# Block sums of values from half blocks on VectorE, put beside the values by ScalarE; one mask built and copied; weight and query loads two deep

## The chip, the cores and the metric

One core of a Trainium2 chip runs the whole program. TensorE (PE) multiplies, VectorE (DVE) and ScalarE (ACT) work on tiles, GpSimd (POOL) does some elementwise work and SyncE (SP) issues every transfer from memory, one after the other. The metric is the device time of one execution in microseconds (us); lower is better.

## What is computed

An attention with two kinds of keys, followed by two feed-forward layers. For 2 batches, 8 heads, 768 positions and head size 64:

```
k_sum = k.reshape(B, H, nb, 32, D).max(axis=3)
v_sum = v.reshape(B, H, nb, 32, D).mean(axis=3)
scores_l = scale * q @ k.T            # only where |i - j| < 16
scores_s = scale * q @ k_sum.T + log(32)
a = softmax(concat([scores_l, scores_s]))
attn = a @ concat([v, v_sum])
x = attn as (1536, 512)
x = ((x @ w_a) * (x @ w_b)) @ w_out          # 512 -> 1536 -> 512
h = x @ w_in                                 # 512 -> 2048
out = maximum(0.01 * h, h) @ w_out2          # 2048 -> 512
```

Each position thus sees its near neighbours and 24 block summaries: the maxima of the keys and the means of the values of blocks of 32.

## The kernel before, in words

Attention works in 24 groups of 256 queries (four windows of 64) for a pair of heads, two groups to a "pair", 12 pairs in all. For a pair, `k_prep` transposes the keys on TensorE, ScalarE copies them into `kts`, VectorE takes the block maxima into `ks`, and the maxima are copied beside the keys of each window. `scores` makes the products; VectorE adds a mask (`negm`, one of three) and takes the row minimum; ScalarE takes the exponential; `normal` (VectorE) divides; `p_transpose` turns the result; `pv` multiplies it with the window's values `vw`, which carry in 24 partitions the block sums of the values. The result becomes `x` (a rounded part and a rest).

The block sums come from `v_sums`: `load_vb` brings half of a batch's heads (96 blocks) as two tiles of 16 positions each, GpSimd adds them in three operations, VectorE reduces the remaining 8 positions in two. `v_place` (TensorE with the identity) brings the 24 sums of each head to the first partitions, and `put_sums` copies them with GpSimd into `vw` for each pair. This happens four times, two for each batch.

Beside attention run the feed-forward layers, whose weights arrive as 68 pieces of 512 KB (`stage`) and are converted by seven small steps each (`convert`: wr, abs, clamp, shift, join, add, high, rest; two on ScalarE, the others on VectorE). A piece is loaded into one of three `wst` tiles. The tokens come in three chunks of 512. Chunk 0's attention runs first with the first weight pieces, chunk 1's is interleaved with chunk 0's products, chunk 2's with chunk 1's, and from then on only products are left. The code gives the order of a list of steps with due numbers (`add(at, ...)`); a scheduler then orders the instructions of each engine, and each engine works its queue strictly in that order.

At the start GpSimd clears the two `vw` tiles, builds the identity and then the three masks, which differ in 16 columns.

Of the kernel before, what the change touches and what calls it, by code (L numbers as in the profile page):

```python
# [21 lines left out]
def kernel(  # L22
# [12 lines left out]
    nc = tc.nc  # L35
# [30 lines left out]
    M1 = 4  # L66
# [5 lines left out]
    wst_p = ctx.enter_context(tc.tile_pool(name="wst", bufs=3))  # L72
# [7 lines left out]
    q_p = att.enter_context(tc.tile_pool(name="q", bufs=3))  # L80
# [38 lines left out]
    HV = H // 2  # L119
    vb_tiles = []  # L120
    for j in range(2):
        t = xp.tile([P, BLK // 2, D], F32, tag="x", name=f"vb{j}")
        vb_tiles.append(t[0 : HV * NB])
# [26 lines left out]
    def load_vb(b, i):  # L150
        while vb_done[0] in bg:
            bg.pop(0)()
        for j, t in enumerate(vb_tiles):
            nc.sync.dma_start(
                out=t,
                in_=v[b, HV * i : HV * (i + 1)].rearrange("h (n j) d -> (h n) j d", j=BLK)[
                    :, j * (BLK // 2) : (j + 1) * (BLK // 2), :
                ],
            )
# [34 lines left out]
    def put_sums(i, p):  # L194
        for j, b, hp, g, n in runs(p):
            nc.gpsimd.tensor_copy(
                out=vw_of[i][W : W + NB, :, j * G : (j + n) * G, :],
                in_=vs_t[b, 2 * hp // HV][:, 2 * hp % HV : 2 * hp % HV + 2, :]
                .unsqueeze(2)
                .to_broadcast([NB, 2, n * G, D]),  # L200
            )
# [5 lines left out]
    def attention_ops():  # L207
# [3 lines left out]
        for i, p in enumerate(sum(pairs, [])):  # L211
# [4 lines left out]
            for m, (b, hp) in enumerate(dict.fromkeys(x[:2] for x in p)):  # L216
                vi, r = divmod(2 * hp, HV)
                if (b, hp) not in seen:
# [4 lines left out]
                    if r == 0:  # L223
                        add(-4, LOAD, load_vb, b, vi)
                        add(-4, SIDE, v_sums, b, vi)
                        add(7, PRODUCT, v_place, b, vi)
# [16 lines left out]
    for t in vw_t:  # L243
        nc.gpsimd.memset(t, 0.0)
# [4 lines left out]
    ident = const.tile([P, P], F32, tag="ident", name="ident")  # L249
    make_identity(nc, ident)  # L250
    negm = []
    for kind in ("first", "mid", "last"):
        t = const.tile([P, P], F32, tag=f"negm_{kind}", name=f"negm_{kind}")
        nc.gpsimd.memset(t, 0.0)
        nc.gpsimd.memset(t[:, W : W + NB], -math.log(BLK))
        nc.gpsimd.memset(t[:, W + NB : SC], BIG)
        for c in range(2):
            for o, c0, c1 in ((0, 0, W), (W, SC, P)):
                loc = t[c * W : (c + 1) * W, c0:c1]

                nc.gpsimd.affine_select(
                    out=loc, in_=loc, compare_op=ALU.is_ge, fill=BIG,
                    base=o - 1, pattern=[[1, c1 - c0]], channel_multiplier=-1,
                )
                nc.gpsimd.affine_select(
                    out=loc, in_=loc, compare_op=ALU.is_ge, fill=BIG,
                    base=2 * WIN - 1 - o, pattern=[[-1, c1 - c0]], channel_multiplier=1,
                )
        if kind == "first":
            nc.gpsimd.memset(t[:, 0:WIN], BIG)  # L270
        if kind == "last":
            nc.gpsimd.memset(t[:, P - WIN :], BIG)
        negm.append(t)
# [4 lines left out]
    units = [(s, c) for s in range(NF1 // M1) for c in range(NC)]  # L278
    slices2 = [(s * M2 + i, c) for s in range(NF2 // M2) for c in range(NC) for i in range(M2)]
    uses = []  # L280
    for s, c in units:
        fs = range(s * M1, (s + 1) * M1)
        uses += [(nm, f) for f in fs for nm in "ab"] + [("o", f) for f in fs]
# [32 lines left out]
    def convert():  # L316
# [13 lines left out]
        def low():  # L330
            t["r"] = wcv_p.tile([P, 512], I32, tag="wr", name="wr")
# [113 lines left out]
    def v_place(b, i):

        v0, done = vb_t.pop((b, i))
# [3 lines left out]
        for h in range(HV):  # L451
            nc.tensor.matmul(
                out=ps[0:NB, h * D : (h + 1) * D],
                lhsT=ident[0 : HV * NB, h * NB : (h + 1) * NB],
                rhs=v0,
                start=True, stop=True,
            )
        vs = sm_p.tile([NB, HV, D], F32, tag="vs", name="vs", bufs=2)
        nc.scalar.activation(
            out=vs, in_=ps[0:NB, : HV * D].rearrange("p (h d) -> p h d", h=HV),  # L460
            func=AF.Copy, scale=1.0 / BLK,
        )
        vs_t[b, i] = vs

    def k_prep(b, hp, j):

# [366 lines left out]
```

## Time and profile before

| | us |
|---|---|
| median of 3 runs (660.76 to 661.89) | 660.8 |
| the profiled execution, whole | 661.53 |
| its span on the core | 659.8 |
| TensorE busy | 636.2 (96%) |
| VectorE busy | 418.1 (63%) |
| ScalarE busy | 270.8 (41%) |
| GpSimd busy | 48.5 (7%) |

The profiled execution is 1.7 us longer than its span (661.53 against 659.8). Busy shares of the whole say little here: the kernel has a first part of some 100 us with attention, and a long rest of products alone, with other limits.

### The profile page before, as it was taken

The numbers are of one execution on the slowest core, as the hardware profiler recorded it, in microseconds if no ns is written. First come the engines' busy times: TensorE is split into PE (matmuls) and PEld (weight loads), VectorE is DVE, ScalarE is ACT, GpSimd is POOL, SyncE is SP. The second block draws the span as 40 slices with busy tenths as digits, with TensorE's granted clock in tenths as the row PEclk, the third lists the DMA queues.
The fourth block names the chain that finished last, engine by engine and source line by source line (L and its number), as shares of the span: only waits on it lengthen the run. The fifth ranks groups of instructions, "written<-read, shape, count | busy, mean of one in ns | idle before, by whom it ended". The sixth has DMA issues, their size and how long they took to land.

```text
span 659.8 us, 9339 instructions
## 1 busy us (share of the span) xinstructions
PE 636.2 (96%) x3440; PEld 519.3 (79%) x3440; DVE 418.1 (63%) x952; ACT 270.8 (41%) x609; POOL 48.5 (7%) x79
## 2 busy tenths in 40 slices
PE   5797989999999999999999999999999999999997
PEld 4576767777888888888888888888888888888886
DVE  3999889955999962699623869732279532422323
ACT  3776787653545421344222535322255322222221
POOL 7254042000000000000000000000000000000000
PEclk9898999999999999999999999999999999999999
DMA  8997744512334430244200232400013000100101
GB/s 196 232 224 194 171 106 108 149 25 65 128 129 138 149 96 1 64 129 127 65 0 1 67 93 73 152 1 0 1 56 105 1 0 1 64 1 1 64 1 64
DMA packets 72622, 53.43 MB, mean 81 GB/s; under 512 B 46208, under 2 KB 66688, under 8 KB 72576
## 3 DMA queue, kind: packets, MB, share of 16 engines
q1 hardware_dynamic: 72576, 52.84, 28.0%
q8 instruction: 27, 0.44, 0.3%
q14 instruction: 19, 0.16, 0.1%
HBM read 49.68 MB, written 3.15 MB: 80 GB/s over the span
## 4 chain that ended last, share of the span: by engine, by line
PE 88%; DVE 6%; POOL 2%; DMA 1%; issue 1%; SPq 1%; ACT 0%; POOLq 0%; DVEq 0%
PE ps_t L583 38%; PE ps_c L583 18%; PE ps_a L583 14%; PE ps_b L583 13%; PE ps_t L518 2%; PE ps_t L565 1%; DVE pm L545 1%; PE ps_t L553 1%; DMA vb<-in_v_dram 1%; DVE pm L531 1%; POOL vb L425 1%; PE ps_t L472 1%; SPq L182 1%; DVE sm L543 0%; DVE acc L688 0%
## 5 line engine op out<-in xcount | busy, mean ns | idle before, releaser
L583 PE MATMUL ps_t<-x,wsp 128*128 128x512 f32 x336 | 78.4, 389 | 0.0
L583 PE MATMUL ps_c<-wsp,gs 128*128 128x512 f32 x288 | 75.9, 389 | 0.0
L583 PE MATMUL ps_t<-wsp,gs 128*128 128x512 f32 x288 | 74.7, 389 | 0.0
L583 PEld LDWEIGHTS ps_t<-x,wsp 128*128 128x128 f32 x336 | 63.1, 188 | 13.1
L583 PE MATMUL ps_t<-ys,wsp 128*128 128x512 f32 x288 | 71.9, 389 | 0.0
L583 PE MATMUL ps_a<-x,wsp 128*128 128x512 f32 x252 | 66.0, 399 | 1.8 <-ACT x L575 1.0
L583 PE MATMUL ps_b<-x,wsp 128*128 128x512 f32 x252 | 65.3, 395 | 0.0
L583 PEld LDWEIGHTS ps_t<-wsp,gs 128*128 128x128 f32 x288 | 54.0, 188 | 11.3
L583 PEld LDWEIGHTS ps_c<-wsp,gs 128*128 128x128 f32 x288 | 54.1, 188 | 11.2
L583 PEld LDWEIGHTS ps_t<-ys,wsp 128*128 128x128 f32 x288 | 54.1, 188 | 11.2
L583 PE MATMUL ps_c<-gs,wsp 128*128 128x512 f32 x240 | 61.0, 394 | 0.0
L336 ACT ACTIVATE wc<-wst 128x512 f32<-128x512 f32 x68 | 45.7, 674 | 28.9 <-DVE wsp L365 28.8
L362 ACT CAST wsp<-wc 128x512 fp32r<-128x512 f32 x68 | 42.1, 622 | 34.4 <-DVE wc L357 27.5
L583 PEld LDWEIGHTS ps_a<-x,wsp 128*128 128x128 f32 x252 | 46.8, 190 | 11.9 <-ACT x L575 1.3
L790 DVE SCALAR_TENSOR_TENSOR h<-h,ps_t 128x512 f32<-128x512 f32 x24 | 16.5, 686 | 60.3 <-ACT h L789 60.3
L583 PEld LDWEIGHTS ps_b<-x,wsp 128*128 128x128 f32 x252 | 46.6, 189 | 9.5 <-issue 0.3
L365 DVE TENSOR_TENSOR wsp<-wc,wsp 128x512 fp32r<-128x512 f32 x68 | 46.9, 693 | 8.5 <-ACT wsp L362 8.5
L583 PEld LDWEIGHTS ps_c<-gs,wsp 128*128 128x128 f32 x240 | 44.4, 188 | 9.6 <-DVE wr L332 0.2
L357 DVE CUSTOM_DVE_ANT_0 wc<-wc,wr 128x1024 uint16<-128x1024 uint16 x68 | 48.8, 718 | 0.5
L604 DVE TENSOR_TENSOR gs<-h,gs 128x512 fp32r<-128x512 f32 x48 | 33.1, 690 | 22.8 <-ACT gs L603 22.7
L583 PE MATMUL ps_t<-gs,wsp 128*128 128x512 f32 x192 | 47.5, 389 | 0.0
L351 DVE SCALAR_TENSOR_TENSOR wc<-wst,wc 128x512 int32<-128x512 int32 x68 | 46.6, 688 | 0.3
(94 smaller groups left out, 863.5 us busy)
## 6 DMA issues: line engine op xcount, KB each, us to landing
wst<-in_moe_w_out_dram SPq DMA_DIRECT2D x28, 512.0 KB, 3.3
wst<-in_moe_w_in_dram SPq DMA_DIRECT2D x16, 512.0 KB, 3.7
wst<-in_moe_w_a_dram SPq DMA_DIRECT2D x12, 512.0 KB, 4.4
wst<-in_moe_w_b_dram SPq DMA_DIRECT2D x12, 512.0 KB, 3.7
k<-in_k_dram SPq DMA_DIRECT2D x16, 192.0 KB, 3.6
vb<-in_v_dram SPq DMA_DIRECT2D x8, 384.0 KB, 5.4
out_dram<-acc SPq DMA_DIRECT2D x12, 256.0 KB, 2.0
q<-in_q_dram SPq DMA_DIRECT2D x16, 128.0 KB, 2.9
```

Of the source, the lines that this page charges most:

```text
L182: nc.sync.dma_start(out=t[p0 : p0 + o1 - o0, c, w0:w1, :], in_=src)
L336: nc.scalar.activation(out=t["c"].bitcast(F32), in_=hi_w.bitcast(F32), func=AF.Abs)
L351: nc.vector.scalar_tensor_tensor(out=t["c"], in0=hi_w, scalar=-0x40000000, in1=t["c"], op0=ALU.bitwise_and, op1=ALU.bitwise_or,)
L357: nc.vector.tensor_tensor(out=t["c"], in0=t["c"], in1=t["r"], op=ALU.add)
L362: nc.scalar.copy(out=t["w"][:, 0], in_=t["c"].bitcast(F32))
L365: nc.vector.tensor_tensor(out=t["w"][:, 1], in0=t["c"].bitcast(F32), in1=t["w"][:, 0].bitcast(F32), op=ALU.subtract,)
L425: nc.gpsimd.tensor_tensor(out=a, in0=a, in1=b, op=ALU.add)
L472: nc.tensor.transpose(ps[:, i * P : (i + 1) * P], k2[:, g * (GT // P) + i].rearrange("p c d -> p (c d)"), ident)
L518: nc.tensor.matmul(out=ps[h, w, :], lhsT=qt[h, w * W : (w + 1) * W], rhs=kts[h, (g * G + w) * SC : (g * G + w) * SC + P], start=True, stop ...
L583: nc.tensor.matmul(out=ps, lhsT=w(a), rhs=x(b), start=first and j == 0, stop=last and j == 2)
L604: nc.vector.tensor_tensor(out=t[:, 1], in0=src, in1=t[:, 0].bitcast(F32), op=ALU.subtract)
L790: nc.vector.scalar_tensor_tensor(out=h, in0=h, scalar=0.01, in1=ps, op0=ALU.mult, op1=ALU.max)
```

## The change

1. Block sums: `load_vb` now brings a whole batch at once as three tiles of 128 half blocks (16 positions each); VectorE reduces each tile alone in two operations; TensorE adds the two halves of a block while it places them, with a constant matrix `place`. There are two such rounds instead of four; GpSimd's adds are gone.
2. `put_sums` moves from GpSimd to ScalarE, the copy of the block maxima into `kts` from GpSimd to VectorE.
3. One mask is built by GpSimd; VectorE copies it for the other two and sets 16 columns. The identity is made first, and `vw` is cleared later.
4. To make room, `wst` has two tiles instead of three, the query tiles two instead of three, and `wr` one instead of two.

The M1 lines of the change keep the same groups of four.

```
-    wst_p = ctx.enter_context(tc.tile_pool(name="wst", bufs=3))
+    wst_p = ctx.enter_context(tc.tile_pool(name="wst", bufs=2))
-    q_p = att.enter_context(tc.tile_pool(name="q", bufs=3))
+    q_p = att.enter_context(tc.tile_pool(name="q", bufs=2))
...
+    NV = 2 * H * NB // P
+    vb_tiles = [xp.tile([P, BLK // 2, D], F32, tag="x", name=f"vb{j}") for j in range(NV)]
...
-    def load_vb(b, i):
+    def load_vb(b):
...
+        src = v[b].rearrange("h (n j) d -> (h n) j d", j=BLK // 2)
+        for i, t in enumerate(vb_tiles):
+            nc.sync.dma_start(out=t, in_=src[i * P : (i + 1) * P])
...
-            nc.gpsimd.tensor_copy(
+            nc.scalar.copy(
                 out=vw_of[i][W : W + NB, :, j * G : (j + n) * G, :],
...
+    for i, c0 in ((0, 0), (2, P - WIN)):
+        nc.vector.tensor_copy(out=negm[i], in_=t)
+        nc.vector.memset(negm[i][:, c0 : c0 + WIN], BIG)
...
-            t["r"] = wcv_p.tile([P, 512], I32, tag="wr", name="wr")
+            t["r"] = wcv_p.tile([P, 512], I32, tag="wr", name="wr", bufs=1)
...
+        v0 = sm_p.tile([P, NV, D], F32, tag="v0", name="v0", bufs=1)
         ops = [
-            lambda: add(t0[:, 0:h], t1[:, 0:h]),
-            lambda: add(t0[:, h:], t1[:, h:]),
-            lambda: add(t0[:, 0:h], t0[:, h:]),
+            lambda i=i, d=d: nc.vector.tensor_reduce(
+                out=v0[:, i, d : d + D // 2],
+                in_=vb_tiles[i][:, :, d : d + D // 2].rearrange("p j d -> p d j"),
+                op=ALU.add, axis=AX.X,
+            )
+            for i in range(NV)
+            for d in (0, D // 2)
         ]
...
+        for h in range(H):
+            r0, r1 = 2 * h * NB, 2 * (h + 1) * NB
+            tiles = range(r0 // P, (r1 - 1) // P + 1)
+            for i in tiles:
+                c0 = V0 + (r0 - i * P) // 2
+                nc.tensor.matmul(
+                    out=ps[0:NB, h * D : (h + 1) * D],
+                    lhsT=place[:, c0 : c0 + NB],
+                    rhs=v0[:, i],
+                    start=i == tiles[0], stop=i == tiles[-1],
+                )
...
-            nc.gpsimd.tensor_copy(
+            nc.vector.tensor_copy(
                 out=kts[:, 0:NW, W : W + NB],
```

VectorE in the first microseconds of the program, before: behind the mask additions of the first pair (L531) the two reduces of the value sums (L435) follow, and key maxima (L482) of a later pair of heads.

```order
L531 ISA nb 128x1
L435 TENSOR_REDUCE v_244<-vb_101 96x32 x2
L482 TENSOR_REDUCE ks_97<-ps_t_326 128x16
L482 TENSOR_REDUCE ks_97<-ps_t_347 128x8
L543 TENSOR_SCALAR sm<-sm 128x4
L544 RECIPROCAL sm<-sm 128x4
L545 TENSOR_TENSOR pm<-pm,sm 128x512
L332 TENSOR_SCALAR wr<-wst 128x512
```

The same engine with the change, from the end of the first group's mask additions: the reduces of the first tile of half blocks stand there already, ahead of the second group.

```order
L528 ISA nb 128x1
L428 TENSOR_REDUCE v_198<-vb_101 128x32 x2
L479 TENSOR_REDUCE ks_96<-ps_t_199 128x16
L540 TENSOR_SCALAR sm<-sm 128x4
L479 TENSOR_REDUCE ks_96<-ps_t_207 128x8
L541 RECIPROCAL sm<-sm 128x4
L486 COPY kts_92<-ks_96 128x12x24
L542 TENSOR_TENSOR pm<-pm,sm 128x512
L528 ISA pm,nb<-ps_t_258,negm_mid 128x128
```

Of six reduces for the batch two stand between the first two groups, and the other four behind the second; the copies into `kts` stand on VectorE right behind the maxima.

SyncE's queue before, from the queries of the fourth pair on: the second half of batch 0's value blocks, then queries ahead, keys, and the fourth weight piece (`wst`); the first three were issued earlier.

```order
L142 DMA q<-in_q_dram 128x4x64 x2
L154 DMA vb_101<-in_v_dram 96x1024
L154 DMA vb_102<-in_v_dram 96x1024
L142 DMA q<-in_q_dram 128x2x64 x8
L133 DMA k<-in_k_dram 128x6x64 x2
L310 DMA wst<-in_moe_w_b_dram 128x4x256
L182 DMA vw_99<-in_v_dram 48x64 x2
```

With the change the same stretch holds all of batch 1's value blocks, and the weight piece there is the third; only two were issued ahead of it.

```order
L141 DMA q<-in_q_dram 128x4x64 x2
L154 DMA vb_101<-in_v_dram 128x1024
L132 DMA k<-in_k_dram 128x6x64 x2
L154 DMA vb_102<-in_v_dram 128x1024
L154 DMA vb_103<-in_v_dram 128x1024
L141 DMA q<-in_q_dram 128x2x64 x4
L177 DMA vw_99<-in_v_dram 48x64 x2
L315 DMA wst<-in_moe_w_a_dram 128x4x256
L177 DMA vw_99<-in_v_dram 64x7x64 x2
```

Batch 1's blocks moved ahead of the third and later weight pieces, and the third piece moved behind the fourth pair's queries.

## Rows read from the trace of the kernel before

**Rows 1.** Busy time of each engine by stretch: us, engines' busy us, PEclk, DMA, GB/s

```profile
0.00:10.00 10.00, 4.18 (x20) 3.44 (x22) 2.73 (x16) 3.85 (x10) 8.52 (x45) 1.00 0.86 207
10.00:62.00 52.00, 40.73 (x409) 31.15 (x406) 47.36 (x156) 34.40 (x120) 23.24 (x19) 0.92 0.86 211
62.00:98.00 36.00, 33.10 (x341) 26.62 (x340) 30.57 (x104) 27.31 (x94) 10.47 (x13) 0.97 0.58 145
300.00:400.00 100.00, 100.00 (x443) 82.81 (x442) 62.66 (x115) 35.29 (x59) 0.00 (x0) 1.00 0.19 58
```

**Rows 2.** The chain that ended last: start us, us, what

```profile
9.22 0.42 POOL kts L489
...
9.71 1.99 PE ps_t L518 x16
...
11.82 0.29 DVE pm L531
...
33.71 3.39 POOL vb L425 x2
...
60.58 0.69 PE ps_t L472 x2
...
97.12 0.73 PE ps_a L583 x2
```

**Rows 3.** VectorE's groups from 0 to 62 us: count, busy us, mean ns, idle before

```profile
L545 DVE TENSOR_TENSOR pm<-pm,sm 128x512 f32<-128x512 f32 x9 | 9.5, 1054 | 0.1
L357 DVE CUSTOM_DVE_ANT_0 wc<-wc,wr 128x1024 uint16<-128x1024 uint16 x6 | 5.4, 893 | 0.0
L332 DVE TENSOR_SCALAR wr<-wst 128x512 int32<-128x512 uint32 x6 | 3.3, 553 | 0.0
L543 DVE TENSOR_SCALAR sm<-sm 128x4 f32<-128x4 f32 x9 | 2.9, 326 | 1.6 <-ACT pm L535 1.6
```

**Rows 4.** The same groups later: L545 and L543 98:160, others 220:400

```profile
L545 DVE TENSOR_TENSOR pm<-pm,sm 128x512 f32<-128x512 f32 x8 | 5.5, 689 | 0.1
L543 DVE TENSOR_SCALAR sm<-sm 128x4 f32<-128x4 f32 x8 | 1.3, 164 | 1.1 <-ACT pm L535 1.1
...
L357 DVE CUSTOM_DVE_ANT_0 wc<-wc,wr 128x1024 uint16<-128x1024 uint16 x23 | 15.8, 688 | 0.3
L332 DVE TENSOR_SCALAR wr<-wst 128x512 int32<-128x512 uint32 x23 | 9.7, 422 | 0.6 <-DMA wst<-in_moe_w_in_dram 0.5
```

**Rows 5.** Two of the groups from 62 to 98 us

```profile
L545 DVE TENSOR_TENSOR pm<-pm,sm 128x512 f32<-128x512 f32 x7 | 5.7, 808 | 0.1
L543 DVE TENSOR_SCALAR sm<-sm 128x4 f32<-128x4 f32 x7 | 2.0, 293 | 0.4 <-ACT pm L535 0.4
```

**Rows 6.** Groups from 0 to 160 us that price what is moved

```profile
L435 DVE TENSOR_REDUCE v<-vb 96x32 f32<-96x256 f32 x8 | 4.5, 589 | 0.3 <-POOL vb L425 0.3
L482 DVE TENSOR_REDUCE ks<-ps_t 128x16 f32<-128x512 f32 x8 | 5.4, 679 | 6.3 <-ACT kts L479 6.3
L482 DVE TENSOR_REDUCE ks<-ps_t 128x8 f32<-128x256 f32 x8 | 3.3, 416 | 0.0
L196 POOL COPY vw<-vs 24x1024 f32<-24x1024 f32 x8 | 12.4, 1563 | 47.4 <-PE ps_t L565 44.3 <-ACT vs L459 3.1
L477 ACT COPY kts<-ps_t 128x384 f32<-128x384 f32 x8 | 3.8, 473 | 6.6 <-PE ps_t L472 6.6
L477 ACT COPY kts<-ps_t 128x192 f32<-128x192 f32 x8 | 2.5, 315 | 0.0
```

**Rows 7.** VectorE in order of time: first key maxima; the fourth x

```profile
6.13 1.02 DVE L482 TENSOR_REDUCE ks<-ps_t 128x16 f32<-128x512 f32 x2 [4.65 <-ACT kts L479]
...
63.95 0.69 DVE L576 TENSOR_TENSOR x<-ps_t,x 128x512 fp32r<-128x512 f32 x1
```

**Rows 8.** SyncE's issue of the fourth weight piece; loads' time to landing, from the page

```profile
33.39 0.48 SPq L310 DMA_DIRECT2D wst<-in_moe_w_b_dram  x1
...
wst<-in_moe_w_a_dram SPq DMA_DIRECT2D x12, 512.0 KB, 4.4
```

More of the change, by code (lines that the diff above doesn't have):

```diff
@@ L222, in attention_ops @@
                         add(2 * m + j - 12, PRODUCT, k_prep, b, hp, j)
[L223 to L226, printed above, removed]
+                    if hp == 0:
+                        add(-5, LOAD, load_vb, b)
+                        add(-4, SIDE, v_sums, b)
+                        add(7, PRODUCT, v_place, b)
             add(-14, LOAD, load_q, i, p)
@@ L240, in by_window @@
         return t[:, at : at + NW * SC].rearrange("p (w o) -> p w o", o=SC)
-    for t in vw_t:
-        nc.gpsimd.memset(t, 0.0)
+    ident = const.tile([P, P], F32, tag="ident", name="ident")
+    make_identity(nc, ident)
     for t in kts_t:
@@ L248 @@
         nc.vector.memset(by_window(t)[:, :, W + NB :], 0.0)
[L249 to L253, printed above, removed]
-        nc.gpsimd.memset(t, 0.0)
[L255 to L273, printed above, removed]
@@ L278 @@
-    units = [(s, c) for s in range(NF1 // M1) for c in range(NC)]
+    negm = [
+        const.tile([P, P], F32, tag=f"negm_{kind}", name=f"negm_{kind}")
+        for kind in ("first", "mid", "last")
+    ]
+    t = negm[1]
+    nc.gpsimd.memset(t, 0.0)
+    nc.gpsimd.memset(t[:, W : W + NB], -math.log(BLK))
+    nc.gpsimd.memset(t[:, W + NB : SC], BIG)
+    for c in range(2):
+        for o, c0, c1 in ((0, 0, W), (W, SC, P)):
+            loc = t[c * W : (c + 1) * W, c0:c1]
+            nc.gpsimd.affine_select(
+                out=loc, in_=loc, compare_op=ALU.is_ge, fill=BIG,
+                base=o - 1, pattern=[[1, c1 - c0]], channel_multiplier=-1,
+            )
+            nc.gpsimd.affine_select(
+                out=loc, in_=loc, compare_op=ALU.is_ge, fill=BIG,
+                base=2 * WIN - 1 - o, pattern=[[-1, c1 - c0]], channel_multiplier=1,
+            )
@@ new lines @@
+    for i, c0 in ((0, 0), (2, P - WIN)):
+        nc.vector.tensor_copy(out=negm[i], in_=t)
+        nc.vector.memset(negm[i][:, c0 : c0 + WIN], BIG)
+    for t in vw_t:
+        nc.gpsimd.memset(t, 0.0)
+    V0 = 32
+    place = const.tile([P, P], F32, tag="place", name="place")
+    nc.gpsimd.memset(place, 1.0 / BLK)
+    for base, pattern, mult in ((2 * V0, [[-2, P]], 1), (1 - 2 * V0, [[2, P]], -1)):
+        nc.gpsimd.affine_select(
+            out=place, in_=place, compare_op=ALU.is_ge, fill=0.0,
+            base=base, pattern=pattern, channel_multiplier=mult,
+        )
@@ L279 @@
+    assert sum(M1) == NF1
+    group1 = [range(sum(M1[:s]), sum(M1[: s + 1])) for s in range(len(M1))]
+    units = [(s, c) for s in range(len(M1)) for c in range(NC)]
     slices2 = [(s * M2 + i, c) for s in range(NF2 // M2) for c in range(NC) for i in range(M2)]
@@ L281 @@
     for s, c in units:
-        fs = range(s * M1, (s + 1) * M1)
-        uses += [(nm, f) for f in fs for nm in "ab"] + [("o", f) for f in fs]
+        uses += [(nm, f) for f in group1[s] for nm in "ab"] + [("o", f) for f in group1[s]]
     behind = []
@@ L450, in v_place @@
         ps = at_bank()
[L451 to L463, printed above, removed]
+        for h in range(H):
[3 more added lines that the diff above has]
+                c0 = V0 + (r0 - i * P) // 2
+                assert 0 <= c0 <= P - NB
+                nc.tensor.matmul(
[3 more added lines that the diff above has]
+                    start=i == tiles[0], stop=i == tiles[-1],
+                )
+        vs = sm_p.tile([NB, H, D], F32, tag="vs", name="vs", bufs=2)
+        nc.scalar.copy(out=vs, in_=ps[0:NB].rearrange("p (h d) -> p h d", h=H))
+        vs_t[b] = vs
     def k_prep(b, hp, j):
@@ L641 @@
             o[2]()
[L642 removed]
+            if o[1] == PRODUCT and (bg or cnt["conv"] < N_FIRST) and o[0] > 0:
                 tick(2)
@@ L701, in y_products @@
     def y_products(s, c, gs):
-        ws = [weights(("o", s * M1 + i)) for i in range(M1)]
+        ws = [weights(("o", f)) for f in group1[s]]
+        n = len(ws)
         def add(ps, e, i):
@@ L732 @@
     for s, c in units:
-        todo = range(len(gs), M1)
+        todo = group1[s][len(gs) :]
         pace["bg"] = {(0, 0): 4, (0, 1): 1, (0, 2): 3}.get((s, c), 1.3)
```

58 lines of the change are left out of this document (16 added, 42 removed).

## The prediction

> **What bounds the kernel now.** I read busy time by stretch first. From 300 to 400 us TensorE is busy 100.00 of 100 us at full clock and VectorE 62.66 [rows 1]; there nothing that VectorE, ScalarE or the loads save can show. Only the front can gain. From 10 to 62 us VectorE is busy 47.36 of 52 us, the transfers 0.86 of their time, TensorE 40.73; from 62 to 98 us TensorE has 33.10 of 36 us, VectorE 30.57 [rows 1]. TensorE's busy time overstates its work in the front, where short products stand apart from each other. So the question is by how much the point from which TensorE never waits again comes earlier; every microsecond there goes through to the end, because the rest is products back to back.
>
> The chain that ended last says what leads to that point. It starts on GpSimd, which works through `vw`, the identity and three masks; the first copy of key maxima is queued behind them and runs at 9.22 us, though VectorE had the maxima by 7.15 us (6.13 plus 1.02) [rows 2, 7]. The first scores follow at 9.71 and the first mask addition at 11.82 us [rows 2]. Later the chain passes through GpSimd's value sums at 33.71 us, then VectorE's queue until TensorE starts again at 60.58 us; a second stretch of VectorE's work ends at 97.12 us, and from there on the chain is TensorE [rows 2]. I therefore cut the front into two stages: up to the fourth `x` of chunk 0 (63.95 us, [rows 7]), and from there to 97 us.
>
> The third thing to see is that VectorE's operations are longer while GpSimd works. GpSimd is busy 23.24 us between 10 and 62 us and not at all from 300 to 400 [rows 1]. The normalising product takes 1054 ns on average up to 62 us and 689 ns from 98 to 160; the small addition before it 326 against 164 ns; `add` of the conversion 893 against 688; `wr` 553 against 422 [rows 3, 4].
>
> **The change part by part, first stage.**
>
> Start: the copy into `kts` moves to VectorE, directly behind the maxima. The keys' arrival sets their transposes and does not change. The copy ends at about 7.15 + 0.42 = 7.57 us (GpSimd's own price) instead of 9.64, so all behind it starts 2.1 us earlier. The one mask is needed by 9.7 us; GpSimd has a third of the mask work left and clears `vw` between, so I cost it at nothing, and VectorE's two mask copies fall into its idle start (2.73 us busy in the first 10 [rows 1]). **−2.1.**
>
> GpSimd gone from VectorE's side: nine products at 1054 − 689 = 0.365 (3.3 us), nine small additions at 0.162 (1.5), six `add` at 0.205 (1.2), six `wr` at 0.131 (0.8) [rows 3, 4]. **−6.8.** It could be nothing only if something other than GpSimd stretched them; the same lines at their short durations, where GpSimd rests, speak against it.
>
> Reduces: four of 256 elements in two rounds go, six of 512 come for the batch. A reduce of 256 in this strided form takes 0.589 us, and two in a row start about 0.5 apart. From 256 to 512 elements the contiguous reduce grows by 679 − 416 = 0.263 us [rows 6]: 0.5 + 0.27 = 0.77 each. If the whole were to double, 1.0 each. I take 0.77, since the growth with length is what the rows show directly: 6 × 0.77 − 4 × 0.5 = **+2.6** (with 1.0: +4.0). The Trainium skill, "VectorE: DVE Perf Modes", says in its tier table that a reduce has only the one-element-per-cycle form, and in the section on the errata that the fixed part is about 150 cycles; an estimate by it for 512 elements is 0.69 us, and the sum over both stages would be about 1 us better. Its formula gives 0.42 us for the reduce of 256, against 589 ns measured, so the measurement decides.
>
> Copies into `kts`: four of 288 elements per batch. VectorE has no such row; the reduce of 256 takes 0.42 and `wr` of 512 also 0.42 undisturbed [rows 4, 6]. Between half and all of that: 0.36 each, **+1.4** (0.8 to 1.7).
>
> Conversions: in the new order two closing steps and one `add` of weight pieces that stood ahead of the fourth `x` now stand behind it, 3 × 0.6: **−1.8** here, +1.8 in the second stage.
>
> `put_sums` on ScalarE: a copy grows by (473 − 315) / 192 = 0.82 ns per element [rows 6], so 1024 elements cost 0.473 + 640 × 0.82 ns = 1.0 us (1.56 on GpSimd). Four pairs and the next two waiting make 6 us in this stage, where ScalarE is idle for 52 − 34.40 = 17.6 us [rows 1]. Each copy stands behind the `x` that frees its tile, so it waits for nothing new; behind it are exponentials and key copies. I cost it at nothing; if its cover were gone, 6 us. The 20 placing products against 16 before, some 0.1 us each, are nothing for the same reason.
>
> Loads: this is the price to set against the gain. Up to the fourth weight piece SyncE had issued 7.45 MB in 33.39 us [rows 8], 223 GB/s, which is near what all stretches up to 62 us show (207 and 211, with 0.86 busy [rows 1]). So transfers pace the queue. With two `wst` tiles the third weight piece is no longer fetched early; 8.27 MB stand ahead of it by the shapes in the queue, 1.57 MB of them batch 1's value blocks. It goes out at 8.27 / 0.223 = 37.1 us and lands 4.4 us later [rows 8], 41.5. VectorE's queue up to that piece's `wr`, summed by kinds from the first mask addition (seven groups of mask additions 5.9, six reduces 4.6, three maxima 2.8, three copies 1.1, six normalisations 5.1, two conversions 5.6, two `x` 1.2), is 26.3 us; from 9.7 it is there at 36.0 if nothing waits, so it waits up to 5.5 us. Behind `wr` stand the next mask additions and normalisations; ScalarE's `abs` of that piece waits likewise with exponentials behind it. VectorE's own old idle time of 52 − 47.4 = 4.6 us in this stretch returns here in part. I take **+3.0** (0 to 5.5).
>
> Sum of the first stage: −2.1 − 6.8 + 2.6 + 1.4 − 1.8 + 3.0 = **−3.7**.
>
> **Second stage.** Relief from GpSimd: seven products at 808 − 689 (0.8) and seven additions at 293 − 164 (0.9) [rows 4, 5], −1.7. Batch 1's reduces +2.6, its copies +1.4, the moved conversions +1.8: +4.1. VectorE is idle 36 − 30.57 = 5.4 us here [rows 1], most of it while TensorE sets the pace, and the new reduces stand in that part; about half of it absorbs 2.8. **+1.3.** ScalarE gets 4 us more at 8.7 us idle. With neither cover it is +4.1.
>
> Sum: −3.7 + 1.3 = **−2.4 us**. Against the profiled execution that is 661.5 − 2.4 = 659.1; it lies 0.7 above the median of the runs, so for a median of runs 660.8 − 2.4 = **658.4**.
>
> **The rivals.**
>
> *The loads decide, slower.* The third, fourth and fifth weight pieces each arrive late on an in-order VectorE. For: transfers are already 0.86 busy, and 1.57 MB not needed before 65 us go first. Against: the fourth piece has less ahead of it than VectorE's queue gains meanwhile. Price: 5.5 us at the third piece, 2.5 again at the fifth, 8.0 instead of 3.0, so +2.6 in the end: 663.4. It decides when the third piece lands more than about 5.5 us after VectorE asks for it.
>
> *VectorE only trades.* Reduces at 1.0 each add 1.4 in each stage, and the idle time of the second absorbs little: −2.4 + 2.8 = +0.4, 661.2. For: the strided reduce is already dearer than its length. Against: the growth per element is known.
>
> *Both covers hold.* No new wait for loads (−3.0) and all of the second stage absorbed (−1.3): −6.7, 654.1. For: VectorE idles in the second stage as long as TensorE leads; against: transfers are near their rate.
>
> **How the numbers follow.** 0.2% is 1.3 us, about what a measurement of this kernel can tell from no change. My forecast (−1.4 to −5) has a chance of 0.45, both covers 0.10, the trade 0.20, the loads 0.25. Faster 0.55, within 0.2% 0.20, slower 0.25. The range goes from a little below the case in which both covers hold, 653.5, to a little above that of the loads, 664.0. The likeliest one's own range is 655.8 to 659.4.
>
> **What would show it.** The first mask addition near 9.7 us; the normalising product near 690 ns in the front; reduces of 0.8 to 0.9 us each, twelve of them; `put_sums` near 1.0 us on ScalarE; a wait of VectorE's `wr` for the third weight piece around 37 to 41 us; the fourth `x` near 60 us; TensorE without gaps from about 94 us. The prediction fails if `wr` or `abs` waits are much longer than 3 us together, if ScalarE becomes full from 20 to 60 us, or if TensorE gets gaps behind 100 us from the two-deep loads.

## The result: slower, 667.39 us against 661.35

| | before | after |
|---|---|---|
| median | 661.35 | 667.39 |
| runs | 660.76 to 662.15 (4) | 667.03 to 667.46 (4) |
| span of the profiled execution | 659.8 | 665.3 |

The ratio is 1.0089 with a 95% interval of 1.0070 to 1.0107. The forecast was 658.4; the time lies above its range (653.5 to 664.0) and on the side of the rival "the loads decide, slower" (663.4), beyond that too.

Busy time by stretch, after, the same stretches as [rows 1] (us, then PE, PEld, DVE, ACT, POOL busy, PEclk, DMA, GB/s):

```profile
0.00:10.00 10.00, 4.61 (x28) 3.93 (x29) 2.77 (x22) 2.87 (x6) 5.23 (x22) 1.00 0.86 227
10.00:62.00 52.00, 42.29 (x417) 32.56 (x416) 44.74 (x164) 42.55 (x138) 0.00 (x0) 0.93 0.77 203
62.00:98.00 36.00, 28.36 (x269) 22.06 (x269) 29.10 (x93) 23.69 (x75) 0.00 (x0) 0.91 0.43 111
...
300.00:400.00 100.00, 100.00 (x443) 82.81 (x442) 62.99 (x115) 33.84 (x56) 0.00 (x0) 1.00 0.20 64
```

Nothing changed from 300 to 400 us. Up to 62 us VectorE is less busy, 44.74 against 47.36, and ScalarE more, 42.55 against 34.40. From 62 to 98 us every engine is *less* busy than before: TensorE 28.36 instead of 33.10. Nobody is full; somebody waits for somebody. That is where the time went.

VectorE after, in order of time: the first mask addition, batch 0's second row of reduces, and the fourth `x`, which closes the first stage ([rows 2, 7] for before):

```profile
9.77 0.29 DVE L528 CUSTOM_DVE_ANT_0 pm<-ps_t,negm_first 128x128 f32<-128x128 f32 x1 [2.15 <-PE ps_t L515]
...
15.29 3.81 DVE L428 TENSOR_REDUCE v<-vb 128x32 f32<-128x512 f32 x4
...
60.63 0.66 DVE L573 TENSOR_TENSOR x<-ps_t,x 128x512 fp32r<-128x512 f32 x1
```

The fourth `x` came at 63.95, now at 60.63: the first stage gained 3.3 us, where −3.7 was forecast. The span grew by 5.5 (665.3 − 659.8), so all behind the fourth `x` lost 8.8, where +1.3 was forecast.

The chain that ended last, after, through that loss (start us, us, what):

```profile
64.69 0.03 SPq L315
64.72 0.03 issue
64.75 5.79 DMA wst<-in_moe_w_b_dram
...
70.63 0.07 ACT wc L341
70.69 0.50 issue
71.19 0.61 ACT gs L600
71.80 0.02 issue
71.83 0.69 DVE gs L601
...
75.21 1.29 DVE v L428 x2
...
77.95 2.82 DVE v L428 x3
80.77 0.08 DVE sm L540
80.85 0.59 DVE wc L356
81.44 0.08 DVE sm L540
81.52 0.60 DVE ks L479
82.12 0.04 issue
82.17 0.69 PE ps_t L469 x2
```

Read it downwards. A weight piece is issued at 64.75 and lands at 70.5. ScalarE's `abs` (L341) of that piece stands at the head of its queue, and behind it the cast of `gs` (L600), whose data are ready; VectorE's `gs` (L601) waits for that cast. Then VectorE works off mask additions and batch 1's six reduces (L428) in one row, and only behind them the key maxima (L479) that free the PSUM bank which TensorE needs next. What TensorE sees of it:

```profile
75.59 0.71 PE L580 MATMUL ps_b<-x,wsp 128*128 128x512 f32 x2
82.17 0.69 PE L469 MATMUL ps_t<-ident,k 128*128 128x128 f32 x2 [5.87 <-DVE ks L479]
82.83 1.97 PE L515 MATMUL ps_t<-kts,qt 64*64 64x128 f32 x16
...
89.26 1.09 PE L515 MATMUL ps_t<-kts,qt 64*64 64x128 f32 x16
```

It stands for 5.87 us, and the sixteen score products right behind the gap take 1.97 us instead of 1.09: the granted clock is 0.81 on average from 80 to 98 us and 0.50, the lower of the two levels, from 82 to 86. From 62 to 98 us TensorE idles 36 − 28.36 = 7.6 us (2.9 before), and the clock, 0.91 against 0.97, takes at most another 36 × 0.06 = 2.2 (an estimate; part of the slow time falls into the gap itself). Together up to 4.7 + 2.2 = 6.9 of the 8.8; the rest this view does not place.

The kernel before has a gap of the same kind, at the end of its first stage, and there too the clock falls behind it (0.50 from 62 to 64 us):

```profile
60.58 0.69 PE L472 MATMUL ps_t<-ident,k 128*128 128x128 f32 x2 [3.91 <-DVE ks L482]
```

The change took that gap away and put a longer one later. TensorE's last wait ends at 91.97 us now and at 97.12 us before, so the point from which it never waits again did come earlier. The kernel is slower all the same, because TensorE had less behind it by then: up to 98 us it was busy 4.61 + 42.29 + 28.36 = 75.3 us, before 78.0, which is half of the 5.5 us.

### The profile page after: what moved, and what is told of

The parts are those of the page before. It is cut to its first block, busy times and chain, and to the rows that moved or that the text cites. A ratio compares the mean times of both kernels' runs of the same rounds, so it can differ in the third digit from the quotient of the medians.

```text
span 665.3 us, 9283 instructions
## 1 busy us (share of the span) xinstructions
PE 638.8 (96%) x3448; PEld 520.3 (78%) x3448; DVE 417.3 (63%) x968; ACT 281.6 (42%) x623; POOL 5.2 (1%) x22
## 4 chain that ended last, share of the span: by engine, by line
PE 89%; DVE 5%; ACT 2%; DMA 2%; issue 1%; POOL 1%; SPq 0%; POOLq 0%; ACTq 0%; DVEq 0%
PE ps_t L580 37%; PE ps_c L580 18%; PE ps_a L580 13%; PE ps_b L580 13%; PE ps_t L515 3%; DMA wst<-in_moe_w_b_dram 2%; DVE v L428 1%; PE ps_t L562 1%; PE ps_t L550 1%; ACT pm L532 1%; DVE pm L528 1%; PE ps_t L497 1%; DVE wc L356 0%; DVE acc L685 0%; DVE pm L542 0%
## 5 line engine op out<-in xcount | busy, mean ns | idle before, releaser
L341 ACT ACTIVATE wc<-wst 128x512 f32<-128x512 f32 x68 | 45.7, 675 | 52.9 <-DMA wst<-in_moe_w_out_dram 12.1
L601 DVE TENSOR_TENSOR gs<-h,gs 128x512 fp32r<-128x512 f32 x48 | 33.1, 691 | 22.8 <-ACT gs L600 22.7
L362 DVE CUSTOM_DVE_ANT_0 wc<-wc,wr 128x1024 uint16<-128x1024 uint16 x68 | 46.6, 685 | 0.6
```

The costliest lines, as they stand in the source:

```text
L341: nc.scalar.activation(out=t["c"].bitcast(F32), in_=hi_w.bitcast(F32), func=AF.Abs)
L362: nc.vector.tensor_tensor(out=t["c"], in0=t["c"], in1=t["r"], op=ALU.add)
L601: nc.vector.tensor_tensor(out=t[:, 1], in0=src, in1=t[:, 0].bitcast(F32), op=ALU.subtract)
```

## The experiments

Three things in the changed kernel can lengthen that stretch: the two `wst` tiles (**late pieces**), batch 1's six reduces (**the row**), and `put_sums` on **ScalarE**. The first theory was the row, its rival the late pieces; ScalarE came third. All ratios are against the kernel before on the same chip. A summary first (the wait is TensorE's longest between 62 and 98 us of the profiled execution, with what ended it; the kernels marked * leave work out). "Cast" is ScalarE's step that writes a converted weight piece to `wsp`, "closing step" VectorE's last step on it.

| run | ratio, 95% interval | longest wait, us | ended by |
|---|---|---|---|
| the changed kernel | 1.0089 (1.0070–1.0107) | 5.87 | key maxima |
| three deep | 0.9980 (0.9968–0.9992) | 2.95 | key maxima |
| batch 1 reuses sums * | 1.0006 (0.9983–1.0028) | 1.62 | cast |
| early reduces | 1.0011 (0.9995–1.0027) | 3.82 | cast |
| before, two deep | 1.0012 (0.9995–1.0028) | 1.2 | `x` |
| three deep + reuse * | 0.9914 (0.9880–0.9947) | under 0.2 | – |
| three deep, row split | 0.9971 (0.9948–0.9993) | 1.23 | key maxima |
| put_sums on GpSimd | 0.9993 (0.9973–1.0013) | 2.72 | closing step |
| before, new start | 0.9993 (0.9973–1.0013) | 1.0 | normalising product |
| no late put_sums * | 1.0031 (1.0015–1.0047) | 6.75 | cast |
| q three deep | 1.0040 (1.0020–1.0059) | 5.82 | cast |
| three deep + put_sums on GpSimd | 0.9985 (0.9973–0.9998) | 3.61 | key maxima |
| the same, row split | 0.9977 (0.9962–0.9992) | 1.23 | key maxima |
| three deep, batch 1 folded on GpSimd | 1.0034 (1.0021–1.0047) | 2.92 | cast |
| two deep, batch 1 folded on GpSimd | 1.0077 (1.0057–1.0096) | 2.69 | cast |
| three deep, folded, put_sums on GpSimd | 0.9893 (0.9869–0.9917) | 0.4 | – |
| three deep, folded, batch 1's put_sums on GpSimd | 0.9919 (0.9894–0.9945) | 0.7 | normalising product |
| two deep, folded, put_sums on GpSimd | 0.9962 (0.9950–0.9974) | 1.30 | normalising product |
| three deep, folded, put_sums on GpSimd, again | 0.9924 (0.9901–0.9947) | 0.4 | – |

**Row or late pieces.** Three deep:

```
-    wst_p = ctx.enter_context(tc.tile_pool(name="wst", bufs=2))
+    wst_p = ctx.enter_context(tc.tile_pool(name="wst", bufs=3))
```

> The changed kernel with three wst tiles again instead of two (q stays at two, wr at one). Block theory (batch 1's six reduces stand in one row on VectorE ahead of the key maxima that free TensorE's banks; TensorE stands for 5.87 us and its clock falls behind that): the row of reduces is still there, so TensorE still waits 4 to 6 us at the key transposes, and the time is 664 to 667. Load theory (the weight pieces that go out late, landing at 57.5 and 70.5 us, leave VectorE and ScalarE idle, and the reduces only fill the hole): no wait of abs for wst over 0.5 us between 50 and 75 us, and the time falls to 657 to 661.

Batch 1 takes batch 0's sums:

```
 def v_sums(b):
+    if b:
+        vb_t[b] = vb_t["first"]
+        return
...
-    vb_t[b] = v0, ops[-1]
+    vb_t[b] = vb_t["first"] = v0, ops[-1]
```

> The changed kernel without the six reduces of batch 1, which takes batch 0's sums again (work left out; the loads of batch 1's value blocks stay). Block theory: TensorE's wait of 5.87 us at 76 us is under 1.5 us, the clock stays at 1.00 from 80 to 100 us, and the time falls by 6 to 9 us, to 658 to 661. Load theory: VectorE waits for the late weight pieces as before and the reduces were filler: 665 to 667.5. Their bare price of 12 halves by twelve, 6 x 0.93 = 5.6 us, would give 661.8 if VectorE alone set the pace.

Batch 1's load and reduces earlier:

```
-    add(-5, LOAD, load_vb, b)
-    add(-4, SIDE, v_sums, b)
+    add(-5 - 12 * b, LOAD, load_vb, b)
+    add(-4 - 12 * b, SIDE, v_sums, b)
```

> The changed kernel with batch 1's load of value blocks and its six reduces due 12 steps earlier, so that the reduces stand between 133 and 157 of VectorE's queue in pieces of one to three instead of in one row at 210. No work is left out. Block theory: TensorE's wait before the key transposes shrinks to under 2 us, part of the 5.6 us of reduces is paid in the first stage instead (fourth x 2 to 5 us later than 60.63), clock stays full from 80 to 100: 660 to 664. Load theory: the late pieces still leave their holes, and the first stage is longer: 667 to 670.

The kernel before with only the tiles cut:

```
-    wst_p = ctx.enter_context(tc.tile_pool(name="wst", bufs=3))
+    wst_p = ctx.enter_context(tc.tile_pool(name="wst", bufs=2))
...
-    q_p = att.enter_context(tc.tile_pool(name="q", bufs=3))
+    q_p = att.enter_context(tc.tile_pool(name="q", bufs=2))
...
-            t["r"] = wcv_p.tile([P, 512], I32, tag="wr", name="wr")
+            t["r"] = wcv_p.tile([P, 512], I32, tag="wr", name="wr", bufs=1)
```

> The kernel before with only the loads two deep: two wst tiles, two q tiles, one wr tile. Block theory: the loads cost little by themselves, 660 to 663. Load theory: abs and wr wait for wst as in the changed kernel, 5 us or more in 50 to 75 us, and the time is 665 to 669. The prediction's own term was +3.0 (0 to 5.5) in the first stage.

Neither theory had it alone. Three deep gave back 0.0109 of the time (7.2 us of 661), though the row is still there; no reduces gave back 0.0083 (5.5, to 662.84 us, between the two theories' ranges), though the pieces are as late as before. TensorE with three deep:

```profile
74.50 1.64 PE L580 MATMUL ps_b<-x,wsp 128*128 128x512 f32 x6
79.08 0.44 PE L469 MATMUL ps_t<-ident,k 128*128 128x128 f32 x2 [2.95 <-DVE ks L479]
```

The same place, half the wait: VectorE comes to the row at 72.02 instead of 75.13. And ScalarE without the reduces:

```profile
66.76 0.67 ACT L341 ACTIVATE wc<-wst 128x512 f32<-128x512 f32 x1 [2.42 <-DMA wst<-in_moe_w_a_dram]
70.76 0.66 ACT L341 ACTIVATE wc<-wst 128x512 f32<-128x512 f32 x1 [2.34 <-DMA wst<-in_moe_w_b_dram]
```

The late piece stops `abs` as in the changed kernel, and yet TensorE waits 1.62 us at most. So the gap of 5.87 is two delays behind each other on VectorE's queue, less TensorE's work in hand, and the clock fell on top: 0.81 from 80 to 98 us in the changed kernel, 1.00 with three deep, 0.91 without the reduces. Early reduces do all the work, and in time (663.31 us, 1.0011) and in the wait for key maxima, which is gone, they do as row theory said. Not as it said are the fourth `x`, no later than before (60.68), and a new wait:

```profile
78.11 1.22 PE L580 MATMUL ps_b<-x,wsp 128*128 128x512 f32 x2 [3.82 <-ACT wsp L367]
```

That is the cast of a weight piece whose `abs` had waited 2.64 us for its load. In the kernel before, two deep is not told from nothing in time, though an `abs` waits for its piece there too (1.38 us at 76.03).

**Do they add up, and is a split row better.** Three deep and reuse joined:

```
-    wst_p = ctx.enter_context(tc.tile_pool(name="wst", bufs=2))
+    wst_p = ctx.enter_context(tc.tile_pool(name="wst", bufs=3))
...
 def v_sums(b):
+    if b:
+        vb_t[b] = vb_t["first"]
+        return
...
-    vb_t[b] = v0, ops[-1]
+    vb_t[b] = vb_t["first"] = v0, ops[-1]
```

> The changed kernel with three wst tiles and without batch 1's six reduces (it takes batch 0's sums again; work left out). Taken alone the two edits gave back 6.6 and 4.6 us. Separate costs: the two add up, 655 to 657. One gap (the late piece and the row of reduces stand in a row ahead of the same key maxima, TensorE has some microseconds of cover, and whatever is taken off first ends the gap): little more than the better of the two, 658 to 660.5, with no wait of TensorE over 1.5 us between 70 and 85 us.

Three deep, and batch 1's load and reduces due 4 steps earlier:

```
-    wst_p = ctx.enter_context(tc.tile_pool(name="wst", bufs=2))
+    wst_p = ctx.enter_context(tc.tile_pool(name="wst", bufs=3))
...
-    add(-5, LOAD, load_vb, b)
-    add(-4, SIDE, v_sums, b)
+    add(-5 - 4 * b, LOAD, load_vb, b)
+    add(-4 - 4 * b, SIDE, v_sums, b)
```

> The changed kernel with three wst tiles and batch 1's reduces due 4 steps earlier; they stand as four and two in VectorE's queue instead of six in a row. No work is left out. Row theory (what is left of TensorE's wait at the key transposes with three tiles, 2.95 us, comes from the six standing in one row): that wait is under 1 us and the time 657 to 660. If only the amount of VectorE's work counts: 660 to 662, as with three tiles alone.

Joined: 656.90 us, ratio 0.9914, against 1.0089 a gain of 0.0175; the single gains sum to 0.0192 (by the ratios; the 6.6 and 4.6 us of the forecast are differences of the bare times). They add up, or nearly, and not in "one gap". With the row split into four and two the wait at the key transposes is 0.70 us, the longest 1.23; 659.77 us, but its interval overlaps that of three deep alone.

**ScalarE, and the start.** `put_sums` back on GpSimd:

```
-            nc.scalar.copy(
+            nc.gpsimd.tensor_copy(
                 out=vw_of[i][W : W + NB, :, j * G : (j + n) * G, :],
```

> The changed kernel with put_sums on GpSimd again, loads still two deep. ScalarE theory (the 12 copies of 0.6 to 1.0 us that went to ScalarE delay the abs and the exponentials, and so the stall): 660 to 664. If ScalarE's added work is off the path, as the prediction has it (costed at nothing): 666 to 670, the copies on GpSimd stretching VectorE's operations in the front by some 2 us in all.

The kernel before with the start of the change alone (identity first, one mask built, `vw` cleared behind it):

```
...
+    for i, c0 in ((0, 0), (2, P - WIN)):
+        nc.vector.tensor_copy(out=negm[i], in_=t)
+        nc.vector.memset(negm[i][:, c0 : c0 + WIN], BIG)
...
-            nc.gpsimd.tensor_copy(
+            nc.vector.tensor_copy(
                 out=kts[:, 0:NW, W : W + NB],
```

> The kernel before with the new start alone: identity first, one mask built and copied, vw cleared behind it, the copy of key maxima into kts on VectorE. The prediction's terms: first mask addition at 9.7 us instead of 11.82, -2.1 and up to +1.4 for the copies; GpSimd's block sums stay. 658.5 to 660.5. If what is won at the start is lost again in the waits of the front: 660.5 to 662.

GpSimd's `put_sums` gave back 0.0096 (6.3 us) with the loads still two deep, as ScalarE theory said. But the edit moved other things too: the six reduces stand as three, two and one on VectorE there, and up to 96 us `abs` waits only once for a piece, 0.81 us. So this run does not separate ScalarE's share from the other two. The new start alone: the first mask addition at 9.54 us as forecast, the fourth `x` at 64.78 (63.95 before), no gain that can be told. VectorE is busy 50.17 of 52 us from 10 to 62 us there (47.36 before); that a head start is used up ahead of such a full engine is the likely reading, which no run tests.

**Controls.** `put_sums` for the first two pairs only; and `q` instead of `wst` three deep:

```
 def put_sums(i, p):
+    if i > 1:
+        return
```

> The changed kernel with put_sums for the first two pairs only; the windows of later pairs keep those sums (work left out). Nothing goes to GpSimd in its place. If ScalarE's copies set the pace of the first stage from 40 to 56 us, as moving them to GpSimd showed (fourth x at 57.61 instead of 60.63), the fourth x is at 57 to 58.5 us here too and the time 659 to 662. If that gain came from another order of the queues or from GpSimd, the fourth x stays at 60 to 61 and the time at 665 to 668.

```
-    q_p = att.enter_context(tc.tile_pool(name="q", bufs=2))
+    q_p = att.enter_context(tc.tile_pool(name="q", bufs=3))
```

> The changed kernel with three q tiles again; wst stays at two, and the six reduces still stand in one row. It separates the depth of the weight tiles from that of the query tiles, and is a control for a mere change of order. If the weight tiles are the cause: abs still waits for wst 2 us or more in 50 to 75 us, and the time is 665 to 668. If query loads at the head of SyncE's queue held the weight pieces back: 659 to 662.

Without late `put_sums` the fourth `x` is at 57.38 as ScalarE theory said, though the time, 664.12 us, is above its range; but with `q` three deep, and ScalarE's copies in place, it is at 58.10: the fourth `x` is not proof against ScalarE. (In the changed kernel the conversion of a late piece stands ahead of it; in these two it fell behind.) Both keep two `wst` tiles and the reduces, five or six in a row, and both keep a gap as long, 6.75 and 5.82 us, but another operation ends it. With `q` three deep:

```profile
78.00 1.22 PE L580 MATMUL ps_b<-x,wsp 128*128 128x512 f32 x2 [5.82 <-ACT wsp L367]
```

Here it is the `add` of a weight piece that stands on VectorE behind the row (71.04 to 76.70), and the cast behind that `add`. The row delays whatever stands behind it; which operation that is depends on the order. The control also bounds what a third query tile and the changed order that comes with it are worth together: some 3 us (665.70, ratio 1.0040 against 1.0089). It does not tell the one from the other.

**Joined with ScalarE.** Three deep and `put_sums` on GpSimd, then the same with the row split:

```
-    wst_p = ctx.enter_context(tc.tile_pool(name="wst", bufs=2))
+    wst_p = ctx.enter_context(tc.tile_pool(name="wst", bufs=3))
...
-            nc.scalar.copy(
+            nc.gpsimd.tensor_copy(
                 out=vw_of[i][W : W + NB, :, j * G : (j + n) * G, :],
```

> The changed kernel with three wst tiles and put_sums on GpSimd; the row of six reduces stays. Alone the two edits gave back 7.2 and 6.3 us. If the late piece and ScalarE's copies are separate costs: 654 to 657. If both cure the same stall: 659 to 661.

```
-    add(-5, LOAD, load_vb, b)
-    add(-4, SIDE, v_sums, b)
+    add(-5 - 4 * b, LOAD, load_vb, b)
+    add(-4 - 4 * b, SIDE, v_sums, b)
```

> As the last one, with batch 1's reduces due 4 steps earlier, so that they stand as four, one and one in VectorE's queue. All work is done. Row theory: 1 to 3 us faster than the last one; if only the amount of VectorE's work counts: the same within 1 us.

Not separate this time: 661.63 and 661.21 us, no better than three deep alone. In the first the row is still there, and TensorE waits 3.61 us for the key maxima behind it; in the second the row is split and the wait is 1.23 us, and the time is the same within 1 us, against row theory. With GpSimd's copies (7.65 us from 10 to 62 us) VectorE is busy 48.08 us in that stretch, against 45.91 with three deep alone.

**All the work done without the row.** Batch 1's sums folded on GpSimd, with three and with two `wst` tiles:

```
 def v_sums(b):
...
+    if b:
+        def fold(i, n):
+            t = vb_tiles[i]
+            nc.gpsimd.tensor_tensor(
+                out=v0[:, i] if n == 1 else t[:, 0:n],
+                in0=t[:, 0] if n == 1 else t[:, 0:n],
+                in1=t[:, 1] if n == 1 else t[:, n : 2 * n], op=ALU.add,
+            )
+        ops = [lambda i=i, n=n: fold(i, n) for i in range(NV) for n in (8, 4, 2, 1)]
     bg[0:0] = ops
```

> The changed kernel with three wst tiles, and batch 1's block sums folded on GpSimd (twelve additions of 512, 256, 128 and 64 elements) instead of VectorE's six reduces; batch 0's stay on VectorE, put_sums on ScalarE. All work is done. If the two causes of the stall (late pieces, row of reduces) are what the changed kernel lost, this comes near the run that had three tiles and no reduces of batch 1 (0.9914): 655 to 658, no wait of TensorE over 1.5 us between 62 and 85 us. If GpSimd stretches VectorE as much as it relieves it, it stays at the 0.998 of three tiles alone, 659.5 to 661.5.

> The same folding on GpSimd with two wst tiles, as in the changed kernel: only the late pieces stay. If each cause makes some 3 us of TensorE's gap of 5.87 us: a wait of TensorE of 1.5 to 3.5 us between 70 and 82 us, and 661 to 664. If the late pieces alone make the whole stall: 665 to 668.

With three tiles this was to come near 0.9914 and came to 1.0034 (665.11 us): the theory of two causes fell. With two tiles it is slower still, 668.79 us, above both forecasts: `abs` waits 1.78 and 2.22 us for pieces there, TensorE 2.12 us at the key transposes (78.92) and 2.69 us for a cast. So the late pieces stop TensorE without the row too, and cost 3.7 us in this pair. With three tiles the gap at the key transposes is gone, and a new one stands at 88.51. ScalarE with three deep and folding:

```profile
83.49 0.62 ACT L191 COPY vw<-vs 24x512 f32<-24x512 f32 x1
...
84.62 0.62 ACT L191 COPY vw<-vs 24x512 f32<-24x512 f32 x1
...
85.78 0.61 ACT L191 COPY vw<-vs 24x512 f32<-24x512 f32 x1
...
87.20 0.62 ACT L191 COPY vw<-vs 24x512 f32<-24x512 f32 x1
87.84 0.62 ACT L367 CAST wsp<-wc 128x512 fp32r<-128x512 f32 x1
```

and TensorE:

```profile
88.51 1.22 PE L589 MATMUL ps_a<-x,wsp 128*128 128x512 f32 x2 [2.92 <-ACT wsp L367]
```

VectorE finished that piece's `add` at 84.07 (83.38 + 0.69); its cast waits behind exponentials and four copies to 87.84. In the run with three deep and reuse, which has the same copies on ScalarE, the cast stood ahead of them:

```profile
77.26 0.62 ACT L367 CAST wsp<-wc 128x512 fp32r<-128x512 f32 x1
...
86.10 2.18 ACT L191 COPY vw<-vs 24x512 f32<-24x512 f32 x4
```

Same operations, same engine, and no wait: what counts is which queued operation stands behind them. The last question was then put to two kernels, with all or only batch 1's `put_sums` on GpSimd:

```
-            nc.scalar.copy(
+            nc.gpsimd.tensor_copy(
                 out=vw_of[i][W : W + NB, :, j * G : (j + n) * G, :],
```

> Three wst tiles, batch 1's block sums folded on GpSimd, and put_sums on GpSimd too; all work is done. The run before it (three tiles, folding, put_sums on ScalarE) had no gap of TensorE at the key transposes any more but a new one of 2.92 us at 88 us, behind four put_sums copies of 0.62 us on ScalarE, and lay at 1.0034. If ScalarE's copies are that next limit: no wait of TensorE over 1.5 us between 80 and 95 us, and 657 to 661. If GpSimd's work brings VectorE's long operations back by as much: 662 to 665.

```
-            nc.scalar.copy(
+            (nc.gpsimd.tensor_copy if b else nc.scalar.copy)(
                 out=vw_of[i][W : W + NB, :, j * G : (j + n) * G, :],
```

> The same, but only batch 1's put_sums on GpSimd; batch 0's stay on ScalarE, so that the first stage is as in the run before it. If ScalarE's copies of batch 1 are the next limit: the gap of 2.92 us at 88 us gone and 660 to 663; if not: 664 to 666.

0.9893 and 0.9919 (656.44 and 657.99 us, both below their forecasts): with these queues ScalarE's copies of batch 1 are a third cost. They are not one in every order: three deep + reuse leaves them on ScalarE and stands at 0.9914. TensorE waits nowhere over 0.8 us between 62 and 98 us, and the clock there is 1.00 in both. Both do all the work and are faster than the kernel before. With the first as a base the loads can be priced once more, two deep beside three deep:

```
-    wst_p = ctx.enter_context(tc.tile_pool(name="wst", bufs=3))
+    wst_p = ctx.enter_context(tc.tile_pool(name="wst", bufs=2))
```

> As the run with batch 1's sums and put_sums on GpSimd, but with two wst tiles as in the changed kernel: only the two-deep loads are left of the three suspects. If late weight pieces are a cost of their own: abs waits for wst 1.5 us or more at least once between 50 and 75 us, and the time lies 3 to 7 us above the three-deep run beside it. If they cost only together with the row of reduces or with ScalarE's copies: within 1.5 us of it.

> Three wst tiles, batch 1's block sums and put_sums on GpSimd, once more, beside the two-deep one on the same chip: 0.987 to 0.992 of before, as measured first (0.9893).

Side by side 659.60 and 656.79 us, with intervals that do not meet: two deep costs 2.8 us here. That late pieces do it, this pair does not show. Its forecast for late pieces as a cost was a wait of `abs` of 1.5 us or more between 50 and 75 us; the only wait of `abs` for a piece up to 100 us is this one:

```profile
75.94 0.68 ACT L341 ACTIVATE wc<-wst 128x512 f32<-128x512 f32 x1 [0.51 <-DMA wst<-in_moe_w_b_dram]
```

And 2.8 us is no more than the 3 us of the control. TensorE from 62 to 98 us, two deep:

```profile
62.00:98.00 36.00, 34.04 (x343) 26.64 (x341) 33.53 (x122) 29.04 (x98) 4.72 (x5) 1.00 0.52 133
```

and three deep:

```profile
62.00:98.00 36.00, 35.54 (x372) 28.21 (x372) 31.65 (x117) 28.78 (x100) 4.36 (x5) 1.00 0.56 137
```

TensorE idles 1.5 us more, half of the difference.

## Why the prediction was wrong

**The start, −2.1.** Right in place and size: first mask addition at 9.77 us, forecast 9.7. Whether it reaches the fourth `x` is another matter; alone, in the kernel before, it did not.

**GpSimd's relief, −6.8.** The stretching is gone, as the step says. VectorE's groups from 0 to 62 us, after, for [rows 3]:

```profile
L542 DVE TENSOR_TENSOR pm<-pm,sm 128x512 f32<-128x512 f32 x10 | 6.8, 684 | 0.0
...
L428 DVE TENSOR_REDUCE v<-vb 128x32 f32<-128x512 f32 x6 | 5.8, 1020 | 0.0
...
L362 DVE CUSTOM_DVE_ANT_0 wc<-wc,wr 128x1024 uint16<-128x1024 uint16 x6 | 4.1, 685 | 0.0
...
L337 DVE TENSOR_SCALAR wr<-wst 128x512 int32<-128x512 uint32 x6 | 2.5, 420 | 0.0
...
L540 DVE TENSOR_SCALAR sm<-sm 128x4 f32<-128x4 f32 x10 | 1.6, 164 | 1.2 <-ACT pm L532 1.2
L486 DVE COPY kts<-ks 128x288 f32<-128x288 f32 x4 | 1.2, 306 | 0.0
```

684, 685, 420 and 164 ns instead of 1054, 893, 553 and 326.

**Reduces, 0.77 each.** Too cheap. Four in a row took 3.81 us, six 5.64: 0.94 to 0.95 each, near the upper bound of 1.0. The strided reduce nearly doubles with its length; the growth of the contiguous one did not carry over. The estimate of 0.69 from the Trainium skill, "VectorE: DVE Perf Modes", section on the errata, was further off; the measurement decides. Over two rounds that is 12 × 0.17 = 2.0 us. The `kts` copies were dearer in the forecast than in the trace (0.36 against 0.31).

**Conversions, −1.8.** Right: ahead of the fourth `x` stand five `add` and four closing steps on VectorE, where there were six of each.

**Late loads, +3.0, all in the first stage.** The step that failed in place. The third piece was issued at 32.82, not 37.1 (the 8.27 MB ahead of it went out at 252 GB/s, not 223), and up to 50 us ScalarE never waits for a piece. The waits came at later ones:

```profile
57.55 0.68 ACT L341 ACTIVATE wc<-wst 128x512 f32<-128x512 f32 x1 [1.39 <-DMA wst<-in_moe_w_b_dram]
...
70.63 0.66 ACT L341 ACTIVATE wc<-wst 128x512 f32<-128x512 f32 x1 [2.55 <-DMA wst<-in_moe_w_b_dram]
```

These are the sixth and the eighth. The eighth hit the second stage, for which the sum had no term for loads. What two deep costs in all depends on what stands beside it: 7.2 us in the changed kernel, 3.7 and 2.8 us in the other pairs; that 2.8 is close to 3.0 is luck. So is in part the first stage, −3.3 for −3.7: the reduces were 1.0 us dearer there, the waits shorter and elsewhere.

**Second stage, +1.3.** The step that failed most; all behind the fourth `x` lost 8.8 us. It is this step: "the new reduces stand in that part; about half of it absorbs 2.8". VectorE's idle time was added up, 5.4 us, without asking where in the queue the reduces stand. They did not go into it. They stand in one row, ahead of the key maxima that free TensorE's banks, and VectorE comes to them 3 us late besides:

```profile
71.83 0.69 DVE L601 TENSOR_TENSOR gs<-g,gs 128x512 fp32r<-128x512 f32 x1 [3.03 <-ACT gs L600]
...
75.13 5.64 DVE L428 TENSOR_REDUCE v<-vb 128x32 f32<-128x512 f32 x6
80.70 0.15 DVE L540 TENSOR_SCALAR sm<-sm 128x4 f32<-128x4 f32 x1
...
81.44 0.68 DVE L479 TENSOR_REDUCE ks<-ps_t 128x16 f32<-128x512 f32 x1
```

The order of the changed kernel, which was to be had before, shows that row.

**`put_sums` on ScalarE, nothing.** Its price per copy was right (1044 ns, forecast 1.0 us), the conclusion wrong: "it waits for nothing new", true; "behind it are exponentials and key copies" left out the casts of weight pieces. With three tiles and batch 1 folded, moving batch 1's copies off ScalarE took the ratio from 1.0034 to 0.9919.

**The rivals.** "The loads decide" had the right sign and half of the mechanism, a late piece; "it decides when the third piece lands more than about 5.5 us after" was the wrong piece. No rival had two delays behind each other, or a fall of the clock behind a long gap.

**What stays open.** Shown is the gap of 5.87 us: a late piece and the row, one behind the other, with each taken away alone and both together. ScalarE's copies are shown as a cost where a cast stands behind them, not by themselves in the changed kernel. The shares are open, for the costs do not add: singly taken away they gave 7.2, 5.5 and 6.3 us, all three 1.0089 − 0.9924 = 0.0165, 10.9 us. Every edit also moves other instructions, and the control with its 3 us does not separate that. Why folding with ScalarE's copies ended at 1.0034 is shown in the main: against the run with batch 1's copies on GpSimd, TensorE is busy 31.73 instead of 34.45 us from 62 to 98 us, at a clock of 0.95 instead of 1.00. By an estimate from these (2.7 us and 36 × 0.05 = 1.8) that is 4.5 of the 7.4 us between the two spans (663.5 and 656.1).

## What to carry to other kernels

Idle time of an engine absorbs new work only if the work stands in the queue where the idle time is: look up what stands right behind each added operation, and who waits for that. Price a shallower buffer at every load that it delays, not at the first. The moment of TensorE's last wait is a poor yardstick by itself; count the work done by then as well. When several changes are made at once and the sum of their small terms is near zero, the order of the queues can decide the sign; here folding batch 1's sums on a resting GpSimd, moving `put_sums` back to it and keeping three weight tiles turned 1.0089 into 0.9893 and, measured again, 0.9924.

## What the runs showed of the hardware that was not expected

The strided reduce costs 0.59 us for 256 elements [rows 6] and 0.94 for 512 in a row, while the contiguous one goes from 0.416 to 0.679. A copy of 288 elements takes VectorE 0.31 us alone and 1.17 us beside GpSimd's additions (the new start in the kernel before, at 12.87 us). Behind TensorE's gap of 5.87 us the same sixteen products took 1.97 instead of 1.09 us; behind 2.95 us (three deep) they took 1.09. The length of the gap alone does not decide that. Behind 2.92 us (three deep, batch 1 folded) the clock did fall, to 0.58 (columns as in the first view; PEclk is the third from the end):

```profile
88.00:90.00 2.00, 1.49 (x6) 0.84 (x8) 1.57 (x4) 2.00 (x8) 0.00 (x0) 0.58 0.19 42
```

With `put_sums` on GpSimd, three deep and the row split, the products took 1.97 us behind two waits of only 1.21 and 1.23 us:

```profile
76.29 1.97 PE L515 MATMUL ps_t<-kts,qt 64*64 64x128 f32 x16 [1.23 <-DVE ks L479]
```

And executions of one kernel on one chip spread, in part with the clock they get: three deep with the row split, from 657.61 us at a mean of 1.000 to 662.43 at 0.989, but also from 659.44 to 662.17 at 0.991.
